# The first batch's x in whole-width loads, a quarter of the weights' conversion in the middle stage, and the last units' sums on VectorE

## The chip, the cores and the metric

The kernel runs on one core of a Trainium2 chip. The metric is the device time of one execution in microseconds (us); the median of several runs is given. The engines are called by the names that the profile uses: PE (the matrix multiplier), DVE (VectorE), ACT (ScalarE), POOL (GpSimd) and SP (the queue that issues most transfers). A line such as L545 is a line of the kernel's file.

## The reference

A global filter over the sequence, and then a two-layer network whose activation is h - tanh(h):

```python
# x (8, 3008, 256) f32; filt_r, filt_i (1505, 256) f32; w_in (256, 2048), w_out (2048, 256) f64
X = np.fft.rfft(x, axis=1)
y = np.fft.irfft(X * (filt_r + 1j * filt_i)[None], n=3008, axis=1).astype(np.float32)
x2 = y.reshape(8 * 3008, 256)
h = x2 @ w_in
g = h - np.tanh(h)
out = (g @ w_out).astype(np.float32)      # (24064, 256)
```

The weights come as 64-bit floats. The kernel reads them as pairs of 32-bit words and makes 32-bit floats of them by integer operations.

## The kernel before, in words

**The filter.** 3008 = 64 x 47, so a sequence position is 47 q + r with q of 64 and r of 47, and the two transforms become three stages of matmuls. The *first* stage is a 64-point transform over q, for each r (matmul `pf`, copied to `a`, written to a buffer `ct1` in device memory). The *middle* stage reads `ct1` back with r on the partitions (`a<-ct`), does the 47-point step (`pz`), multiplies by the filter (`uv`, `zs`, on DVE), goes back over r (`pe`, copied to `e1s`), and writes `ct2`. The *last* stage reads `ct2` (`e<-ct`) and does the 64-point step back (`pu`, copied to `ut`). The batches are handled in the units (0), (1,2), (3,4), (5,6), (7).

**The network.** Tokens are taken in 48 groups of up to 512, and each group in four units of hidden columns, 192 in all. Both matrix products are done with seven products of half-size blocks in place of eight (Strassen and Winograd), which needs sums of blocks on both sides. `combine` (L523 to L527) makes the four sums of a moving operand: for a group's `ut` it gives `tu`, for a unit's `h` it gives `t`. All its subtractions are on POOL, but for one of the last unit (L526), which is on DVE. `sums` (L257 to L263) makes the four sums of a quarter of a weight, on POOL. The hidden activation goes over ACT (L619 to L630) and DVE (L626, L633); `up`, `shrink` and `down` are the three steps of a unit, and PE's L545 and L680 are the products of the two layers. The main loop keeps PE full; the first and middle stages of the later batches are fitted into it by a list of due steps.

**The prologue.** Only batch 0's first and middle stage, the weights' conversion and the first group's last stage stand ahead of the main loop. The order of the work is that of the program, engine by engine (the scheduling is manual):

- On SP: the matrix `wf1`, the loads of x for r below 24 (`load_x0`, L873), matrices `fg`, then the raw weights. The loads of x for r from 24 on are issued by ACT. The one set of 64 rows lies on partitions 0 to 63, the other on 64 to 127, and a chunk holds eight r of each; the first chunk comes in two cuts.
- `first0` (L878 to L901) does the first stage for three chunks: a matmul over both halves with a block matrix of `wf1` (L891), a copy by ACT (L894), two writes to `ct1` by ACT (L898). In the last chunk the second half is one r shorter, so matmul and copy are split there, and the row that is missing is filled with zeros by POOL (`pad`, L945 to L947).
- `weights_alone` converts three quarters of a weight, two jobs each, all on DVE (L204 to L230), ahead of the middle stage in DVE's order. A job's load (`raw`, L197) is issued by SP; there are three buffers.
- The middle stage then goes through 16 steps of `j`. Each step also calls the generator `weights` once, which does six more jobs with two of the operations on ACT (L216, L217). At j = 13 two jobs of one more quarter are begun. What is left of the jobs is finished after the loop. The filter's rows come by POOL's loads (L910) and are doubled by ACT (L914, L915); `turned` (L923, L924) makes a second matrix on POOL.
- After the loop: `e2` is loaded, the remaining jobs are finished, `pu` and `ut` follow, then `tu`, and the first product L545.

**The end.** After the last unit's activation, `bounded` (L776 to L786) counts on DVE, from sums that the activation left, whether a bound held (`small`, L781; `least`, L783), and PE adds it up over the partitions (`pc`, L785). PE runs its queue in order, so what follows `pc` waits for `least`.

Of the kernel before, what the change touches and what calls it, by code (L numbers as in the profile page):

```python
# [9 lines left out]
F32 = mybir.dt.float32  # L10
# [12 lines left out]
NQ, NR = 64, 47  # L23
# [3 lines left out]
RP = 48  # L27
# [39 lines left out]
def _consts():  # L67
# [10 lines left out]

    wf1 = np.zeros((2, 128, 64, 2))
    for b in range(2):  # L80
        wf1[0, 64 * b:64 * b + 64, :, b] = f1
        wf1[1].reshape(128, 2, 64)[64 * b:64 * b + 64, b] = f1
# [47 lines left out]
    for b in range(2):  # L130
# [9 lines left out]
            for v in (wf1, fg.reshape(IM + RP, -1), s2, np.eye(128))]  # L140
# [3 lines left out]
def kernel(  # L144
# [11 lines left out]
    wf1_d, fg_d, s2_d, one_d = (  # L156
        nc.inline_tensor(v, name=n).ap() for v, n in zip(_consts(), ("wf1", "fg", "s2", "one")))
# [342 lines left out]
    def last(i, z):  # L500


        p, c = groups[i]
        ws_ = widths(p, c)
        n = sum(ws_)
        e2 = e2s.pop(i)
        ut = dn.tile([128, 2, CH * 128], F32, tag="ut", bufs=2, name="ut")
        for h in range(2):
            pu = z("pu", [128, CH * 128])
            for j, w in enumerate(ws_):  # L510
                nc.tensor.matmul(pu[:, j * 128:j * 128 + w], e2[0:w, j, h * 128:(h + 1) * 128],  # L511
                                 s2[0:w, 0:w], start=True, stop=True)
            ACT.copy(ut[:, h, 0:n], pu[:, 0:n])
            if h == 0:
                yield
        w = n // 2
        tu = dn.tile([128, 4, 256], F32, tag="tu", bufs=2, name="tu")
        b = [[ut[:, h, k * w:(k + 1) * w] for k in range(2)] for h in range(2)]
        combine(b, [tu[:, k, 0:w] for k in range(4)])
        uts[i] = (b, tu, w)  # L520
        yield

    def combine(b, t, shared=False):  # L523
        G.tensor_sub(t[0], b[0][1], b[0][0])  # L524
        G.tensor_sub(t[1], b[1][1], t[0])  # L525
        (V if shared else G).tensor_sub(t[2], b[1][1], b[0][1])  # L526
        G.tensor_sub(t[3], t[1], b[1][0])  # L527
# [79 lines left out]
    def shrink(U):  # L607
# [46 lines left out]
        combine(blocks, [t[:, k, :, 0:w] for k in range(4)], U + 1 == 4 * len(groups))  # L654
# [121 lines left out]
    def bounded(z):  # L776


        small = tr.tile([128, 2 * 4 * len(groups)], F32, tag="a2", bufs=2, name="small")
        least = cst.tile([128, 1], F32, name="least")  # L780
        V.tensor_single_scalar(out=small, in_=y_sums, scalar=float(np.arctan(S * NEAR) ** 2),  # L781
                               op=ALU.is_lt)
        V.tensor_reduce(out=least, in_=small, axis=mybir.AxisListType.X, op=ALU.min)  # L783
        pc = z("pc", [1, 1])
        nc.tensor.matmul(pc, least, ones, start=True, stop=True)  # L785
        V.tensor_copy(count, pc)  # L786

# [68 lines left out]
    with tc.tile_pool(name="tr", bufs=2) as tr, tc.manual_schedule():  # L856
        with tc.tile_pool(name="pro", bufs=1) as pro, \
# [11 lines left out]
            def load_x0(c, cuts=(0, 8)):  # L869
                t = big([128, 8, DM], F32, "x0")  # L870
                for lo, hi in zip(cuts, cuts[1:]):
                    for h, rows, r, n in halves(0, 8 * c + lo, hi - lo):
                        (nc.sync, ACT)[h].dma_start(  # L873
                            t[rows, lo:lo + n, :],
                            dram(x.tensor, r * DM, [[NR * DM, 64], [1, n * DM]]))
                return t

            def first0(xt, c):  # L878

                for i in range(2):  # L880
                    r = 8 * c + 4 * i
                    a1 = pro.tile([128, 4, DM], F32, tag="a1", bufs=4, name="a1")
                    parts = halves(0, r, 4)
                    m = parts[1][3]
                    for j in range(2):
                        pf = z0("pf", [128, 2, DM])
                        lo, mid, hi = 2 * j, max(2 * j, min(2 * j + 2, m)), 2 * j + 2
                        for rows, lo, hi in ((128, lo, mid), (64, mid, hi)):
                            if lo < hi:
                                to = pf[0:rows, lo - 2 * j:hi - 2 * j, :]  # L890
                                nc.tensor.matmul(to, wf1[0:rows, 1, 0:rows],  # L891
                                                 xt[0:rows, 4 * i + lo:4 * i + hi, :],
                                                 start=True, stop=True)
                                ACT.copy(a1[0:rows, lo:hi, :], to)  # L894
                        if j == 0:
                            yield
                    for _, rows, r_h, n_h in parts:
                        ACT.dma_start(  # L898
                            dram(ct1[0], r_h * 64 * DM, [[DM, 64], [64 * DM, n_h], [1, DM]]),
                            a1[rows, 0:n_h, :])  # L900
# [35 lines left out]
            nc.sync.dma_start(wf1, wf1_d)  # L936
# [28 lines left out]
            G.dma_start(s2, s2_d)  # L965
            turned(mats[0][1], gx[0])
# [7 lines left out]
            ws = weights(tiles0, range(3, 6), 2)  # L974
# [63 lines left out]
        with tc.tile_pool(name="dn", bufs=2) as dn, \  # L1038
# [42 lines left out]

            late, copies = weights_slow(tiles1, range(7, 8)), filters_d()
# [4 lines left out]
            for U in range(total + 2):  # L1087
# [120 lines left out]
```

## Time and profile before

| | us |
|---|---|
| median of 7 runs | 2805.2 (2804.85 to 2809.74) |
| the profiled execution | 2806.02 |
| its span | 2804.2 |
| PE busy in the span | 2719.7 (97%) |
| DVE busy | 1913.4 (68%) |
| ACT busy | 1885.6 (67%) |
| POOL busy | 1766.8 (63%) |

The span is what the profiler's records cover; the profiled execution is 1.8 us longer. The page gives the span in 40 slices of 70.1 us, in tenths of busy time. The mean granted clock of PE is 0.99 of full speed. The stretch ahead of PE's full load ends at about 126 us, and the span's last 10 us hold the last products, the transposes and the stores.

In the lines of a timeline the columns are start and duration in us, engine, line, operation, output and inputs, shapes and the number of merged instructions; what stands in brackets is how long the engine had been idle and what ended that. The chain of waits follows the work that ended last back to its start, here shown in the order of time.

### The profile page before, as it was taken

To read this page: it belongs to the slowest core of one execution; us is meant where nothing else is said; L and a number is where in the kernel's file an instruction comes from. 1 tells how busy PE (TensorE), PEld (TensorE's weight loads), DVE (VectorE), ACT (ScalarE), POOL (GpSimd) and SP (SyncE) were. 2 spreads that over 40 slices of the span, in tenths; PEclk is the share of its full clock that TensorE was granted. 3 is DMA by queue.
4 is the path that set the end of the run, shared out by engine and by line. 5 is a ranking of instruction groups with operands and counts; after the bars stand their busy time and mean duration, and the time that the engine had idled before them with its cause. 6 is when DMAs were issued, how large, how long until landed. Compare 5 with 4: busy or idle time off the path is not lost.

```text
span 2804.2 us, 36463 instructions
## 1 busy us (share of the span) xinstructions
PE 2719.7 (97%) x12438; PEld 2273.3 (81%) x12438; DVE 1913.4 (68%) x2175; ACT 1885.6 (67%) x2790; POOL 1766.8 (63%) x1407
## 2 busy tenths in 40 slices
PE   4899999999999999999999999999999999999998
PEld 2577778888888888888888888888888888898887
DVE  6755666656776777666677777766676676777776
ACT  2466777666767777666667777766666676666665
POOL 5546887544776777544586777654476666565655
PEclk7999999999999999999999999999999999999999
DMA  9854443332333322223333233112223222111010
GB/s 249 214 185 116 111 118 82 87 87 72 72 75 82 75 69 60 58 84 80 88 72 75 70 80 84 38 43 66 59 66 80 63 57 58 30 19 26 16 22 17
DMA packets 322592, 217.53 MB, mean 78 GB/s; under 512 B 224783, under 2 KB 274747, under 8 KB 322157
## 3 DMA queue, kind: packets, MB, share of 16 engines
q1 hardware_dynamic: 266826, 157.28, 24.1%
q10 hardware_dynamic: 52818, 51.53, 6.0%
q0 software_dynamic: 2752, 6.30, 0.8%
q8 instruction: 100, 1.64, 0.2%
q14 instruction: 96, 0.78, 0.1%
HBM read 138.87 MB, written 79.17 MB: 78 GB/s over the span
## 4 chain that ended last, share of the span: by engine, by line
PE 83%; DVE 6%; ACT 4%; issue 2%; DMA 2%; POOL 2%; ACTq 0%; DVEq 0%; SPq 0%; POOLq 0%
PE o L680 35%; PE x L545 21%; PE z L545 10%; PE y L545 5%; PE pe L411 3%; PE pz L430 3%; PE pu L511 3%; PE pf L351 2%; DVE h L626 2%; ACT y L622 1%; DMA raw<-in_moe_w_in_dram 1%; DVE h L596 1%; ACT y L619 1%; DMA a<-ct 1%; DVE h L633 0%
## 5 line engine op out<-in xcount | busy, mean ns | idle before, releaser
L626 DVE TENSOR_TENSOR h<-h,y 128x1024 f32<-128x1024 f32 (+2 forms) x384 | 578.1, 1505 | 311.4 <-ACT y L622 310.3
L680 PE MATMUL o<-t,wd 128*128 128x256 f32 (+2 forms) x3072 | 775.3, 375 | 1.8 <-POOL t L526 1.3
L680 PEld LDWEIGHTS o<-t,wd 128*128 128x128 f32 x3072 | 579.5, 190 | 93.8 <-issue 22.0
L633 DVE SCALAR_TENSOR_TENSOR h<-sq,h 128x1024 f32<-128x1024 f32 (+2 forms) x384 | 558.5, 1454 | 121.8 <-ACT sq L630 113.7
L524 POOL TENSOR_TENSOR t<-h 128x512 f32<-128x512 f32 (+2 forms) x192 | 240.2, 1251 | 553.3 <-DVE h L633 402.5
L680 PE MATMUL o<-h,wd 128*128 128x256 f32 (+2 forms) x2304 | 583.1, 376 | 4.0 <-DVE h L633 4.0
L545 PE MATMUL x<-tu,wu 128*128 128x256 f32 (+2 forms) x2304 | 582.0, 375 | 4.3 <-POOL tu L525 2.1
L545 PEld LDWEIGHTS x<-tu,wu 128*128 128x128 f32 x2304 | 430.4, 190 | 105.4 <-issue 42.9
L680 PEld LDWEIGHTS o<-h,wd 128*128 128x128 f32 x2304 | 430.7, 190 | 77.7 <-issue 15.8
L630 ACT ACTIVATE sq<-y,near_b 128x1024 f32<-128x1024 f32 (+2 forms) x384 | 435.0, 1133 | 6.4 <-DVE h L633 0.2
L619 ACT ACTIVATE y<-h 128x1024 f32<-128x1024 f32 (+2 forms) x384 | 397.4, 1035 | 14.4 <-ACT e L414 6.4
L622 ACT ACTIVATE y<-y 128x1024 f32<-128x1024 f32 (+2 forms) x384 | 399.9, 1041 | 6.6 <-ACT a L352 0.4
L551 ACT COPY s<-x 128x512 f32<-128x512 f32 (+2 forms) x192 | 110.8, 577 | 328.5 <-PE x L545 308.4
L527 POOL TENSOR_TENSOR t<-t,h 128x512 f32<-128x512 f32 (+2 forms) x192 | 319.0, 1662 | 0.1
L551 ACT COPY u<-x 128x512 f32<-128x512 f32 (+2 forms) x384 | 220.7, 575 | 138.2 <-PE x L545 119.8
L525 POOL TENSOR_TENSOR t<-h,t 128x512 f32<-128x512 f32 (+2 forms) x192 | 245.9, 1281 | 15.0
L526 POOL TENSOR_TENSOR t<-h 128x512 f32<-128x512 f32 (+2 forms) x191 | 245.7, 1286 | 0.0
L446 POOL TENSOR_TENSOR zs<-zs,ft 128x512 f32<-128x512 f32 x112 | 164.9, 1472 | 94.2 <-ACT zs L444 94.0
L447 POOL TENSOR_TENSOR uv<-uv,zs 128x512 f32<-128x512 f32 x112 | 206.7, 1845 | 9.1 <-DVE uv L445 0.5
L545 PE MATMUL x<-ut,wu 128*128 128x256 f32 (+2 forms) x768 | 198.5, 381 | 11.1 <-DVE h L596 8.3
L588 DVE TENSOR_TENSOR h<-z,u 128x512 f32<-128x512 f32 (+2 forms) x192 | 128.8, 671 | 112.6 <-ACT u L551 111.6
L545 PE MATMUL z<-tu,wu 128*128 128x256 f32 (+2 forms) x768 | 195.5, 377 | 0.0
(122 smaller groups left out, 3293.7 us busy)
## 6 DMA issues: line engine op xcount, KB each, us to landing
a<-ct SPq DMA_DIRECT2D x64, 384.0 KB, 4.0
ft<-filt SPq DMA_DIRECT2D x96, 256.0 KB, 4.7
out_dram<-ot SPq DMA_DIRECT2D x1392, 16.0 KB, 1.5
ct<-e ACTq DMA_DIRECT2D x112, 192.0 KB, 2.2
ct<-a ACTq DMA_DIRECT2D x80, 256.0 KB, 2.9
x_sb<-in_x_dram SPq DMA_DIRECT2D x69, 256.0 KB, 2.9
e<-ct SPq DMA_DIRECT2D x33, 512.0 KB, 4.2
fg<-fg SPq DMA_DIRECT2D x40, 392.0 KB, 4.9
```

The lines of the kernel that those rows point to most:

```text
L524: G.tensor_sub(t[0], b[0][1], b[0][0])
L525: G.tensor_sub(t[1], b[1][1], t[0])
L526: (V if shared else G).tensor_sub(t[2], b[1][1], b[0][1])
L527: G.tensor_sub(t[3], t[1], b[1][0])
L545: nc.tensor.matmul(bank[:, k], wu[:, q - 1, (2 * u + k) * 128:(2 * u + k + 1) * 128], rhs[q - 1], start=(first and k == 0), stop=True, ski ...
L551: ACT.copy(t, X)
L619: ACT.activation(y[k], ht[k], AF.Arctan, scale=S)
L622: ACT.activation(y[k], y[k], AF.Square, accum_out=y_sums[:, 2 * U + k // 2:2 * U + k // 2 + 1])
L626: V.tensor_mul(ht[k], ht[k], y[k])
L630: ACT.activation(sq[k], y[k], AF.Square, bias=near_b, scale=A)
L633: V.scalar_tensor_tensor(out=ht[k], in0=sq[k], scalar=K, in1=ht[k], op0=ALU.add, op1=ALU.mult)
L680: nc.tensor.matmul(product(q), wd[:, q - 1, (2 * u + k) * 128: (2 * u + k + 1) * 128], rhs[q - 1][:, k], start=(u == 0 and k == 0 and q == ...
```

## The change

Five edits:

1. Batch 0's x is loaded with 128 partitions in one transfer, all on SP: partition 2q + h holds eight r, from r = 8c for h = 0 and from 24 + 8c for h = 1. The last r of the second half (r = 47) is the first row of the next q. A new matrix `wf0` (64 KB, loaded in front) does the transform from that order; matmul and copy are not split any more, each `ct1` write has four r, and the zero padding with its transfer is left out (the rows are read by matmuls that leave that r out).
2. `wf1` is loaded by POOL's queue, behind `s2`.
3. `weights_alone` has two quarters (four jobs); the generator in the middle stage has four (eight jobs, 20 stops for the same 17 calls, and what is left follows after the loop).
4. `combine` takes its engine: DVE for the first group's `tu` and for the `t` of the last two units, POOL otherwise.
5. `bounded` is a generator: its DVE part is issued at the last unit's step k = 0, before `e()`, and the matmul with the count at k = 2.

```diff
+    wf0 = np.zeros((64, 2, 2, 64))
     for b in range(2):
+        wf0[:, b, b] = f1
...
-        combine(b, [tu[:, k, 0:w] for k in range(4)])
+        combine(b, [tu[:, k, 0:w] for k in range(4)], G if i else V)
...
-    def combine(b, t, shared=False):
-        G.tensor_sub(t[0], b[0][1], b[0][0])
-        G.tensor_sub(t[1], b[1][1], t[0])
-        (V if shared else G).tensor_sub(t[2], b[1][1], b[0][1])
-        G.tensor_sub(t[3], t[1], b[1][0])
+    def combine(b, t, by):
+        by.tensor_sub(t[0], b[0][1], b[0][0])
+        by.tensor_sub(t[1], b[1][1], t[0])
+        by.tensor_sub(t[2], b[1][1], b[0][1])
+        by.tensor_sub(t[3], t[1], b[1][0])
...
-        combine(blocks, [t[:, k, :, 0:w] for k in range(4)], U + 1 == 4 * len(groups))
+        combine(blocks, [t[:, k, :, 0:w] for k in range(4)],
+                G if U + 2 < 4 * len(groups) else V)
...
-    def bounded(z):
+    def bounded():
...
         V.tensor_reduce(out=least, in_=small, axis=mybir.AxisListType.X, op=ALU.min)
-        pc = z("pc", [1, 1])
+        yield
+        pc = z1("pc", [1, 1])
         nc.tensor.matmul(pc, least, ones, start=True, stop=True)
         V.tensor_copy(count, pc)
+        yield
...
                 for lo, hi in zip(cuts, cuts[1:]):
-                    for h, rows, r, n in halves(0, 8 * c + lo, hi - lo):
-                        (nc.sync, ACT)[h].dma_start(
-                            t[rows, lo:lo + n, :],
-                            dram(x.tensor, r * DM, [[NR * DM, 64], [1, n * DM]]))
+                    nc.sync.dma_start(
+                        t[:, lo:hi, :],
+                        dram(x.tensor, (8 * c + lo) * DM,
+                             [[NR * DM, 64], [HALF * DM, 2], [1, (hi - lo) * DM]]))
...
                     for j in range(2):
                         pf = z0("pf", [128, 2, DM])
-                        lo, mid, hi = 2 * j, max(2 * j, min(2 * j + 2, m)), 2 * j + 2
-                        for rows, lo, hi in ((128, lo, mid), (64, mid, hi)):
-                            if lo < hi:
-                                to = pf[0:rows, lo - 2 * j:hi - 2 * j, :]
-                                nc.tensor.matmul(to, wf1[0:rows, 1, 0:rows],
-                                                 xt[0:rows, 4 * i + lo:4 * i + hi, :],
-                                                 start=True, stop=True)
-                                ACT.copy(a1[0:rows, lo:hi, :], to)
+                        nc.tensor.matmul(pf, wf0, xt[:, 4 * i + 2 * j:4 * i + 2 * j + 2, :],
+                                         start=True, stop=True)
+                        ACT.copy(a1[:, 2 * j:2 * j + 2, :], pf)
...
-                    for _, rows, r_h, n_h in parts:
+                    for h in range(2):
                         ACT.dma_start(
-                            dram(ct1[0], r_h * 64 * DM, [[DM, 64], [64 * DM, n_h], [1, DM]]),
-                            a1[rows, 0:n_h, :])
+                            dram(ct1[0], (r + HALF * h) * 64 * DM,
+                                 [[DM, 64], [64 * DM, 4], [1, DM]]),
+                            a1[64 * h:64 * h + 64])
...
-            nc.sync.dma_start(wf1, wf1_d)
+            wf0 = pro.tile([128, 128], F32, name="wf0_sb")
+            nc.sync.dma_start(wf0, wf0_d)
...
-            ws = weights_alone(tiles0, range(3))
-
-            pad = pro.tile([64, DM], F32, name="pad")
-            G.memset(pad, 0.0)
-            G.dma_start(dram(ct1[0], NR * 64 * DM, [[DM, 64], [1, DM]]), pad)
+            ws = weights_alone(tiles0, range(2))
...
             G.dma_start(s2, s2_d)
+            G.dma_start(wf1, wf1_d)
...
-            ws = weights(tiles0, range(3, 6), 2)
+            ws = weights(tiles0, range(2, 6), 2)
...
+            bound = bounded()
...
+                        if U == total + 1 and k in (0, 2):
+                            next(bound)
                         e()
                         t(k)
-                        if U == total + 1 and k == 0:
-                            bounded(z1)
```

More of the change, by code (lines that the diff above doesn't have):

```diff
@@ L139, in _consts @@
     return [np.ascontiguousarray(v, dtype=np.float32)
-            for v in (wf1, fg.reshape(IM + RP, -1), s2, np.eye(128))]
+            for v in (wf0.reshape(128, 128), wf1, fg.reshape(IM + RP, -1), s2, np.eye(128))]
 @with_exitstack
@@ L155 @@
     V, G, ACT = nc.vector, nc.gpsimd, nc.scalar
-    wf1_d, fg_d, s2_d, one_d = (
-        nc.inline_tensor(v, name=n).ap() for v, n in zip(_consts(), ("wf1", "fg", "s2", "one")))
+    wf0_d, wf1_d, fg_d, s2_d, one_d = (
+        nc.inline_tensor(v, name=n).ap()
+        for v, n in zip(_consts(), ("wf0", "wf1", "fg", "s2", "one")))
     ct1 = [nc.dram_tensor(f"ct1_{p}", (RP, 64 * len(bs), DM), F32, kind="Internal")
@@ L882, in first0 @@
                     a1 = pro.tile([128, 4, DM], F32, tag="a1", bufs=4, name="a1")
-                    parts = halves(0, r, 4)
-                    m = parts[1][3]
                     for j in range(2):
                         pf = z0("pf", [128, 2, DM])
-                        lo, mid, hi = 2 * j, max(2 * j, min(2 * j + 2, m)), 2 * j + 2
-                        for rows, lo, hi in ((128, lo, mid), (64, mid, hi)):
-                            if lo < hi:
-                                to = pf[0:rows, lo - 2 * j:hi - 2 * j, :]
-                                nc.tensor.matmul(to, wf1[0:rows, 1, 0:rows],
-                                                 xt[0:rows, 4 * i + lo:4 * i + hi, :],
-                                                 start=True, stop=True)
-                                ACT.copy(a1[0:rows, lo:hi, :], to)
+                        nc.tensor.matmul(pf, wf0, xt[:, 4 * i + 2 * j:4 * i + 2 * j + 2, :],
+                                         start=True, stop=True)
+                        ACT.copy(a1[:, 2 * j:2 * j + 2, :], pf)
                         if j == 0:
                             yield
-                    for _, rows, r_h, n_h in parts:
+                    for h in range(2):
                         ACT.dma_start(
-                            dram(ct1[0], r_h * 64 * DM, [[DM, 64], [64 * DM, n_h], [1, DM]]),
-                            a1[rows, 0:n_h, :])
+                            dram(ct1[0], (r + HALF * h) * 64 * DM,
+                                 [[DM, 64], [64 * DM, 4], [1, DM]]),
+                            a1[64 * h:64 * h + 64])
                     yield
```

## The prediction

> **What bounds the kernel now.** I read the page's busy shares and its chain first, then the chain of waits over the first 150 us, the timelines of the engines there, the table by stretches of the same time, and last the timeline of the end.
>
> The page (busy us; the chain's shares by engine):
>
> ```profile
> PE 2719.7 (97%) x12438; PEld 2273.3 (81%) x12438; DVE 1913.4 (68%) x2175; ACT 1885.6 (67%) x2790; POOL 1766.8 (63%) x1407
> PE   4899999999999999999999999999999999999998
> PE 83%; DVE 6%; ACT 4%; issue 2%; DMA 2%; POOL 2%; ACTq 0%; DVEq 0%; SPq 0%; POOLq 0%
> ```
>
> PE is full but for the first slices (70 us each: 4 tenths, 8 tenths) and the last. What the change does in between shifts nothing; a microsecond is won or lost only before PE's full stretch begins (about 126 us) or after 2778 us. Both ends are what the diff edits. The chain of waits of the first stretch (start, us, what):
>
> ```profile
> 1.18 5.74 DMA x<-in_x_dram
> 6.94 15.14 DMA raw<-in_moe_w_in_dram
> ...
> 39.35 9.25 DMA raw<-in_moe_w_in_dram
> 51.48 6.25 DMA a<-ct
> ...
> 79.75 9.47 DMA a<-ct
> ...
> 120.26 0.84 DVE wd L230 x3
> ...
> 125.25 0.79 POOL tu L525
> 126.09 1.13 PE x L545 x4
> ```
>
> The chain goes through the conversions on DVE, then the middle stage's loads, then conversions, then the sums of `tu` on POOL; only there does PE get its first product. DVE's timeline (start, us, line) shows what holds the first filter multiply L1011:
>
> ```profile
> 41.43 0.42 DVE L204 TENSOR_SCALAR conv<-raw 128x512 int32<-128x512 int32 x1
> 41.77 0.95 DVE L205 TENSOR_SCALAR conv<-raw 128x512 int32<-128x512 int32 x1
> 48.63 0.43 DVE L204 TENSOR_SCALAR conv<-raw 128x512 int32<-128x512 int32 x1 [0.86 <-DMA raw<-in_moe_w_in_dram]
> 52.77 0.68 DVE L1011 TENSOR_TENSOR uv<-pz,filt 128x512 f32<-128x512 f32 x1
> ```
>
> The six jobs of `weights_alone` start at 22.26, 26.41, 30.54, 37.28, 41.43 and 48.63, and the first `uv` is queued behind the sixth, though its first load of `a` has landed by 43.2 us. A job takes 4.15 us, but 6.3 to 6.7 where POOL's sums run beside it: the 0.42 us op takes 0.95. Stretches (us; last two columns the share of the DMA engines and GB/s):
>
> ```profile
> 7.00:15.00 8.00, 5.96 (x8) 2.06 (x8) 0.00 (x0) 2.25 (x4) 4.88 (x7) 1.00 1.02 252
> 60.00:70.00 10.00, 8.43 (x37) 5.91 (x36) 8.60 (x17) 6.54 (x9) 9.83 (x15) 1.00 0.72 198
> 70.00:80.00 10.00, 8.86 (x40) 6.51 (x39) 9.32 (x17) 6.31 (x10) 8.28 (x13) 1.00 1.06 257
> ```
>
> The DMA engines are full in most of this part, so DVE's early freedom can be taken back by transfers. PE's timeline at the end:
>
> ```profile
> 2783.95 1.40 PE L680 MATMUL o<-t,wd 128*128 128x224 f32 x6 [1.30 <-POOL t L526]
> 2785.88 1.02 PE L680 MATMUL o<-t,wd 128*128 128x224 f32 x4 [0.53 <-POOL t L527]
> 2790.56 0.19 PE L785 MATMUL pc<-ones,least 128*1 128x1 f32 x2 [1.95 <-DVE least L783]
> ```
>
> PE waits there for POOL's sums of the last but one unit and for the bound's count: 3.78 us in three waits.
>
> **The change part by part.** Sums are against the profiled execution, 2806.02 us (span 2804.2), 0.8 us above the median of 2805.2.
>
> 1. x over 128 partitions, all on SP. The same bytes (3.1 MB; 64 KB of matrix in place of 128 KB ahead of them, the 128 KB now on POOL's queue later). Two SP issues and four ACT issues become four SP issues of about 0.95 us (3.82 us for four), so SP reaches the raw loads at the same 6.9 us, and ACT is free 2.6 us earlier, when it had 4.2 us of idle time. I keep the rate of 252 GB/s. Then only bytes help: 64 KB of matrix and 64 KB of pad less, 64 KB more of x (row 47 of the second half): raw0, and the first job with it, 0.3 us earlier. Bounds: 3.2 us earlier, were x moved at the 339 GB/s of the 22 to 30 us stretch (12.3 us for 3.1 MB becomes 9.1); 12 us later, were one queue given half of 252. I take the value nearest to the row of x itself.
>  [...]
> 2. Unsplit matmuls and copies in the first stage, two whole ct writes, no pad memset or pad DMA. L894's pieces of 0.36 us and one pair of short matmuls go, off the chain. What ACT waits for there, 2.73 and 2.90 us "<-DMA raw", comes from issue waits of its ct writes on earlier transfers and depends on which loads precede. With x on SP the last ct write goes out about 5 us earlier than 33.65, at 28 to 29, if they follow raw; the first `a` load then lands at about 38 (43.2 before), an estimate with the same 9.6 us from write to landing. Nothing gained by itself: it is next in line after DVE.
> 3. Four jobs instead of six ahead of the middle. The fifth and sixth, 41.43 to 52.77, go: 11.3 us. First `uv` at 52.77 - 11.3 - 0.3 = 41.2. If `a` is not earlier, it is 43.5 and the gain 9.3; the conversion's POOL sums (3.3 us a group) are also one group fewer there.
> 4. Eight jobs instead of six inside the middle. The generator has 20 stops for 17 calls, so per step the same work is done, and the rhythm of two steps (pairs at 60.66, 67.52, 74.20: 6.8 us, POOL 9.83 of 10 busy) stands. But raw loads and filters that moved before 52.77 must now move after 41.2: 1.1 MB more backlog, 4.3 us at 257 GB/s, against 2.8 us of idle DMA at 60 to 70 and 5.7 at 100 to 113. I take 2.5 us lost; bounds 0 (the idle time swallows it) and 8 (below, rival B).
> 5. After the last `zs` (110.04) DVE had 2.0 us of first ops, waited 3.88 for ACT's L216 and finished two jobs in 2.6 us each, at 121.09. Now it has the last two jobs' finishes too (2 x 2.6), the wait shrinks under them: 12.9 us for 11.05 to 11.3, 1.6 lost. Bounds: 0, and 5.2 if the wait stays.
> 6. `tu` on DVE. POOL did it behind its sums of wd (121.17 to 124.49), at 124.49 and 125.25, PE at 126.09, 4.8 us after `ut`. On DVE, four ops of 0.42 to 0.69 follow `ut` directly: first product at ut + 2.7, 2.1 us won; bounds 0 (if DVE's next conversion's 0.95 us ops stand first) and 3.
> 7. wf1 from POOL behind s2: one issue of 0.6 us on POOL's queue at about 34, where `turned` and the filter loads stand behind it; POOL then idles 1.36 and 7.91 us, which hides it. The matrix is used from 126 us on. Cost nothing; without that cover, 0.6.
> 8. The end. The last but one unit's sums start when DVE is through with L604 (2779.2) and take 4 x 0.62, ready at 2781.7 for 2785.8: both PE waits, 1.83 us, go. DVE's next L626 moves from 2779.80 to 2781.7, but the 1.85 to 2.02 us that L633 and L626 took beside POOL return to 1.09; the last h is ready at about 2786.1 (2786.77), and the last sums, 4 x 0.62, at 2788.6 (2790.9). The count's wait of 1.95 goes, as the matmul is asked two steps later. With the last 11 matmul groups of 4.05 us behind 2788, PE ends at about 2792.0 for 2794.73: 2.7 won. Bounds 1 (DVE's 2.5 us push the last h back) and 4.
>
> Sum: -0.3 - 11.3 + 2.5 + 1.6 - 2.1 = -9.6 at the start, -2.7 at the end: -12.3, so 2793.7 against the profiled run and 2792.9 against the median. I forecast 2793.
>
> **Rivals.** B: transfers take most of it back. Up to the pu at 118.6 us, 28.7 MB pass, 242 GB/s on the mean; the full stretches run at 252 to 339, those of 70 to 100 us at 263. To save 10 us the mean must be 264. At 250 the start gains 118.6 - 116 = 2.6 us; with the end, 5.5: about 2799.5. For it: three of the chain's pieces are loads. Against it: 2.8 and 5.7 us of idle engines named above.
> C, slower: ACT's ct writes and SP's loads wait on each other's completions. Before, one pair does this (ACT's write at 89.29 late, then a pair of 9.5 us from 82.51 to 92.00 instead of 6.8): 2.7 us each. With another order of loads other pairs can fall so. To end 0.2% slower, 17.9 us must be lost, that is seven of eight pairs; from five on, the kernel is about unchanged. For it: ACT's L216 shows 2.28 "<-DMA a<-ct". Against: it happened once in eight. Time at seven pairs: 2793 + 18.9 = 2812.
> D, the merge does harm: one queue for x at half the rate, first job 12 us later, the gain of step 3 gone: about 2805. Against it: the page's SP queue alone moved 59.5% of all DMA time to 60 us.
>
> **How the numbers follow.** Changes under 0.2% (5.6 us) can hardly be told from none. Forecast 62%; B 22%, of which 6 end within 0.2%; C 9%, of which 2 do; D 7%, of which a half true leaves 3 faster, 2 the same and 2 slower. Faster: 62 + 16 + 3 = 81%. Same: 6 + 2 + 2 = 10%. Slower: 7 + 2 = 9%. The forecast's own bounds, adding the likelier ones of steps 1, 4, 6 and 8, give 2786 to 2799; B reaches to 2803. Range 2785 to 2803.
>
> **What would show it.** First `uv` (L1011) at 41 us and `a` landed by 39; four jobs ahead of it. Last `zs` at 100 to 101; pairs of 7 us. First product L545 behind `tu` at 115 to 117, released by DVE and no longer by POOL. At the end no PE wait for POOL's sums, none for `least`, the last L680 some 3 us earlier against the start of the last unit. Wrong if raw0 lands after 24 us, if pairs take 8 us or more, if SP's loads stand behind a raw load that waits for a late L223, or if L626 of the last unit becomes the end's wait.

## The result, and the profile after

The changed kernel takes 2799.33 us (median of 14 runs, 2797.57 to 2801.73) against 2805.74 for the kernel before beside it: a ratio of 0.9976, 95% interval 0.9970 to 0.9983. It is 6.4 us faster. The forecast was 12.3 us, so about half of it did not come. The profiled execution took 2799.61 us, with a span of 2797.8 for 2804.2.

The page of the kernel after; the same three lines as of before:

```profile
PE 2721.0 (97%) x12436; PEld 2273.6 (81%) x12436; DVE 1905.5 (68%) x2182; ACT 1889.3 (68%) x2793; POOL 1756.7 (63%) x1395
PE   5899999999999999999999999999999999999998
PE 82%; DVE 7%; ACT 4%; issue 2%; POOL 2%; DMA 2%; ACTq 0%; SPq 0%; DVEq 0%; POOLq 0%
```

Only the first slice has one more tenth of PE. The chain of waits of the first stretch (start, us, what):

```profile
1.18 4.18 DMA x<-in_x_dram
5.38 15.84 DMA raw<-in_moe_w_in_dram
...
45.94 9.16 DMA filt<-in_filt_r_dram
...
60.91 14.12 DMA raw<-in_moe_w_out_dram
...
81.13 7.58 DMA filt<-in_filt_r_dram
...
95.54 1.17 PE pe L989 x2
...
116.64 0.83 DVE wd L234 x3
120.87 2.08 PE x L549 x4
```

The conversions on DVE now end at 40 us and not at 52. In their place stand loads that were issued inside the middle stage and took 7.6 to 14.1 us, two of them POOL's small filter loads. The stretches from 7 us on (last three columns: PE's granted clock, the share of the DMA engines, GB/s):

```profile
7.00:15.00 8.00, 5.67 (x11) 2.26 (x10) 0.00 (x0) 2.25 (x4) 3.67 (x6) 1.00 1.02 275
60.00:70.00 10.00, 6.74 (x27) 4.16 (x25) 8.35 (x17) 4.97 (x7) 6.28 (x10) 0.97 1.07 250
70.00:80.00 10.00, 8.98 (x33) 6.59 (x34) 6.93 (x14) 4.49 (x6) 9.51 (x15) 0.83 1.08 255
```

The slack of 0.72 that the kernel before had between 60 and 70 us is gone: the DMA engines are full from 38 to 90 us, at shares of 1.01 to 1.08. DVE's timeline, the first `uv`, the start of the last pair of steps, and the last `zs`:

```profile
40.37 0.68 DVE L1013 TENSOR_TENSOR uv<-pz,filt 128x512 f32<-128x512 f32 x1
101.78 0.69 DVE L1013 TENSOR_TENSOR uv<-pz,filt 128x512 f32<-128x512 f32 x1 [2.62 <-ACT filt L918]
105.06 0.68 DVE L1014 TENSOR_TENSOR zs<-pz,filt 128x512 f32<-128x512 f32 x1
```

The kernel before ends its middle stage, begun at 52.77, with

```profile
109.36 0.68 DVE L1012 TENSOR_TENSOR zs<-pz,filt 128x512 f32<-128x512 f32 x1
```

The last pair starts 10.2 us after the one before it (91.57). In one table, from the timelines of the two profiled executions:

| us | before | after | difference | forecast |
|---|---|---|---|---|
| first `uv` starts | 52.77 | 40.37 | -12.4 | -11.6 |
| first `uv` to last `zs` | 56.6 | 64.7 | +8.1 | +2.5 |
| last `zs` to `ut` | 12.0 | 15.2 | +3.2 | +1.6 |
| `ut` to the first product of the second layer | 30.0 | 28.2 | -1.8 | -2.1 (as `tu`) |
| from there to the last unit but one's second-layer products | 2627.5 | 2626.4 | -1.1 | 0 |
| from those to the end of the span | 25.4 | 23.0 | -2.5 | -2.7 |
| sum | | | -6.5 | -12.3 |

Of the 12.4 us won ahead of the middle stage, 11.3 are lost again before `ut`. The start and the end came as forecast; the 1.1 us of the main loop were not forecast, and nothing here explains them. The question is what took the 8.1 and the 3.2.

The tables by stretches from the first `uv` to the end of the last `zs` say that it is not more work: DVE was busy for 45.9 us before and 45.8 after, ACT for 29.5 and 31.4, POOL for 49.0 and 47.4, and PE, with 47.5 and 51.8, was full in neither. The bytes are more: 13.4 MB before and 15.3 after, at 234 and 235 GB/s.

### The profile page after: what moved, and what is told of

It reads as the page before. It is cut to its first block, busy times and chain, and to the rows that moved or that the text cites. A ratio compares the mean times of both kernels' runs of the same rounds, so it can differ in the third digit from the quotient of the medians.

```text
span 2797.8 us, 36449 instructions
## 1 busy us (share of the span) xinstructions
PE 2721.0 (97%) x12436; PEld 2273.6 (81%) x12436; DVE 1905.5 (68%) x2182; ACT 1889.3 (68%) x2793; POOL 1756.7 (63%) x1395
## 3 DMA queue, kind: packets, MB, share of 16 engines
q8 instruction: 100, 1.64, 0.3%
## 4 chain that ended last, share of the span: by engine, by line
PE 82%; DVE 7%; ACT 4%; issue 2%; POOL 2%; DMA 2%; ACTq 0%; SPq 0%; DVEq 0%; POOLq 0%
PE o L686 35%; PE x L549 21%; PE z L549 10%; PE y L549 5%; PE pe L415 3%; PE pz L434 3%; PE pu L515 3%; PE pf L355 2%; DVE h L630 2%; ACT y L626 1%; DVE h L600 1%; DMA filt<-in_filt_r_dram 1%; DVE h L637 1%; ACT y L623 1%; DMA raw<-in_moe_w_in_dram 1%
## 5 line engine op out<-in xcount | busy, mean ns | idle before, releaser
L630 DVE TENSOR_TENSOR h<-h,y 128x1024 f32<-128x1024 f32 (+2 forms) x384 | 571.5, 1488 | 311.8 <-ACT y L626 310.4
L637 DVE SCALAR_TENSOR_TENSOR h<-sq,h 128x1024 f32<-128x1024 f32 (+2 forms) x384 | 557.6, 1452 | 124.6 <-ACT sq L634 117.0
L623 ACT ACTIVATE y<-h 128x1024 f32<-128x1024 f32 (+2 forms) x384 | 397.4, 1035 | 15.2 <-ACT e L418 6.4
L626 ACT ACTIVATE y<-y 128x1024 f32<-128x1024 f32 (+2 forms) x384 | 399.9, 1041 | 6.6 <-ACT a L356 0.4
L549 PE MATMUL x<-ut,wu 128*128 128x256 f32 (+2 forms) x768 | 199.5, 382 | 10.8 <-DVE h L600 8.3
L549 PE MATMUL y<-ut,wu 128*128 128x256 f32 (+2 forms) x768 | 194.6, 376 | 0.0
```

What stands on the lines that cost most here:

```text
L549: nc.tensor.matmul(bank[:, k], wu[:, q - 1, (2 * u + k) * 128:(2 * u + k + 1) * 128], rhs[q - 1], start=(first and k == 0), stop=True, ski ...
L623: ACT.activation(y[k], ht[k], AF.Arctan, scale=S)
L626: ACT.activation(y[k], y[k], AF.Square, accum_out=y_sums[:, 2 * U + k // 2:2 * U + k // 2 + 1])
L630: V.tensor_mul(ht[k], ht[k], y[k])
L637: V.scalar_tensor_tensor(out=ht[k], in0=sq[k], scalar=K, in1=ht[k], op0=ALU.add, op1=ALU.mult)
```

## The experiments

The first theory: transfers bound the middle stage, so that what is saved ahead of it is spent in it, and each other part is worth what its stretch shows. The rival: what one queue issues waits by chance for another queue's loads, and the order of the loads decides. The trace of the kernel before has such waits: two of ACT's copies in the first stage came 2.73 and 2.90 us late, behind issues of ACT that raw loads of SP released. That completions are shared is the author's reading of them and not shown.

### One part undone at a time

Three quarters ahead again:

```diff
-            ws = weights_alone(tiles0, range(2))
+            ws = weights_alone(tiles0, range(3))
...
-            ws = weights(tiles0, range(2, 6), 2)
+            ws = weights(tiles0, range(3, 6), 2)
```

> The kernel after, with six conversion jobs ahead of the middle stage again (three quarters, as before); all other edits stay. Theory (transfers bound the middle stage, so what is saved ahead of it is spent inside it): the first uv goes from 40.4 to about 51.5 us, the middle gets 7 to 8 us shorter (from 64.7 us between first uv and last zs to about 57), the tail about 2 us; total within 2 us of the kernel after, 2799 to 2801. Reckoning of the prediction: the part is worth 11.3 - 2.5 - 1.6 = 7.2 us, so 2806.5. Rival (completions that happen to be shared): another order gives another set of stalls, the total may go either way by 5 us, with the middle's pairs irregular.

Measured: 2800.02 us (before beside it 2805.2; ratio 0.9983, 0.9974 to 0.9992), 0.7 slower than the kernel after, less than the two intervals can part. DVE's timeline of this run:

```profile
50.53 0.68 DVE L1013 TENSOR_TENSOR uv<-pz,filt 128x512 f32<-128x512 f32 x1
107.85 0.68 DVE L1014 TENSOR_TENSOR zs<-pz,filt 128x512 f32<-128x512 f32 x1
```

The middle takes 57.3 us again, and `ut` comes 11.7 us after the last `zs`. The quarter moved into the middle stage wins 10.2 us at the first `uv`, costs 7.4 in the middle and 3.5 behind it, and is worth nothing that can be measured. The theory's outcome stands, and the prediction's step 4 falls; what in the middle takes the time this run does not tell.

The end undone:

```diff
-                G if U + 2 < 4 * len(groups) else V)
+                None if U + 1 == 4 * len(groups) else G)
...
+        by, by2 = by or G, by or V
...
-        by.tensor_sub(t[2], b[1][1], b[0][1])
+        by2.tensor_sub(t[2], b[1][1], b[0][1])
...
-                        if U == total + 1 and k in (0, 2):
-                            next(bound)
                         e()
                         t(k)
+                        if U == total + 1 and k == 0:
+                            for _ in bound:
+                                pass
```

> The kernel after, with the end as before: the last but one unit's sums on POOL, three of the last unit's four sums on POOL, and the count's matmul at once behind the DVE part. Theory (the end is worth 2.5 us, the difference between the shift of the end of the span, 6.4, and the shift of the loop ahead of it, 3.9): 2801.8, with PE waits for POOL's sums back near 1.3 and 0.5 us. Rival (PE has slack there, and the end's gain belongs to the clock or to the store): 2799.3, no change.

Measured: 2803.74 us (0.9993, 0.9984 to 1.0002), 4.4 slower than the kernel after. PE's timeline has the three waits of before to the hundredth:

```profile
2778.10 1.40 PE L687 MATMUL o<-t,wd 128*128 128x224 f32 x6 [1.30 <-POOL t L531]
2780.03 1.02 PE L687 MATMUL o<-t,wd 128*128 128x224 f32 x4 [0.53 <-POOL t L532]
2784.72 0.19 PE L793 MATMUL pc<-ones,least 128*1 128x1 f32 x2 [1.95 <-DVE least L790]
2786.14 4.43 PE L687 MATMUL o<-t,wd 128*128 128x224 f32 x14
```

In the kernel after there is one wait instead, of 1.82 us for the last unit's h, and none for the count. In the profile of before the product on `h` behind the count's matmul starts at 2790.68 us, though `h` was ready at 2786.77; in the kernel after the count is asked later and nothing stands behind a wait for it:

```profile
2782.22 2.16 PE L686 MATMUL o<-h,wd 128*128 128x224 f32 x10 [1.82 <-DVE h L637]
2786.96 0.19 PE L792 MATMUL pc<-ones,least 128*1 128x1 f32 x2
```

The last 14 matmuls took 4.43 us here and 2.81 in the profile of before, which has the same waits. The table by stretches of this run shows why: the granted clock was 0.66 from 2786 to 2791 us, where the kernel before has 1.00 over the same matmuls (2791.8 to 2796.9). From the second layer's products of the last unit but one to the end of the last product it is 13.3 us in the kernel after, 16.0 before and 17.6 here. So in the profiles the end is worth 2.7 us, and 4.4 in the execution in which PE's clock fell. That the median's 4.4 comes from such falls is not shown: the profiled execution, which has one, took 2801.94 us, less than the median. The theory's 2.5 had the waits and the direction right.

`tu` on POOL:

```diff
-        combine(b, [tu[:, k, 0:w] for k in range(4)], G if i else V)
+        combine(b, [tu[:, k, 0:w] for k in range(4)], G)
```

> The kernel after, with the first group's tu on POOL again. Theory of the prediction: 2.1 us slower, 2801.4. Rival (PE takes its products on ut first, and what follows waits for the activation, not for tu): within 0.7 us of the kernel after, 2799 to 2800.

Measured: 2798.66 us (0.9977, 0.9968 to 0.9986), 0.7 faster than the kernel after: the outcome of the rival, no effect. PE's timeline of the kernel after:

```profile
117.23 2.53 PE L515 MATMUL pu<-s_sb,e 128*128 128x128 f32 x16 [3.87 <-DMA e<-ct]
120.87 2.08 PE L549 MATMUL x<-ut,wu 128*128 128x256 f32 x4 [1.10 <-ACT ut L517]
122.74 1.91 PE L549 MATMUL y<-ut,wu 128*128 128x256 f32 x4
124.44 1.51 PE L549 MATMUL x<-tu,wu 128*128 128x256 f32 x4
```

The two products on `ut` that PE takes first cost 2.08 and 1.91 us, against 1.13 and 1.03 in the kernel before, so `tu` is ready before PE is. But half clock is not the reason that the move wins nothing. The run with the old end also has `tu` on DVE, PE was at full clock there (1.13 and 1.03 us for the same two products), and its timelines of PE and DVE have:

```profile
122.68 1.11 PE L550 MATMUL x<-tu,wu 128*128 128x256 f32 x4
125.52 1.12 PE L355 MATMUL pf<-x_sb,wf_sb 128*128 128x512 f32 x2 [1.73 <-DVE h L576]
```

```profile
124.78 0.68 DVE L576 TENSOR_TENSOR h<-y,s 128x512 f32<-128x512 f32 x1
```

PE takes its product on `tu` at once and then waits 1.73 us for `h`, which stands on DVE behind the four sums of `tu` and three operations of a conversion. Six profiles with `tu` on DVE have this wait, of 1.64 to 1.74 us. Counted from the start of `ut`, `h` starts after 4.6 us with `tu` on DVE and after 3.7 with it on POOL, where in turn the product on `tu` starts only after 4.6. The `pf` behind both starts after 5.3 us in the run with the old end, 5.6 in the kernel after and 5.6 with `tu` on POOL. What the move takes from one wait it adds to another.

The same stretch of the kernel after by the table:

```profile
120.00:124.00 4.00, 3.13 (x7) 2.52 (x8) 3.05 (x5) 1.66 (x3) 3.35 (x4) 0.50 0.86 198
```

The clock was 0.50 there. PE had waited 3.87 us for `e` before 117.23, and the table gives 1.00 from 113 to 118 us, 0.65 from 118 to 120, then 0.50, and 1.00 again from 126. The kernel before has the same dip, at 0.50 from 128 to 130 us, behind waits of 1.34 us for `ut` and 2.14 for `tu`; and in the run with `gx` on ACT (below) a wait of 3.81 us for `e` brought none: the 16 products of `pu` behind it took 2.02 us, as in the kernel before at a clock of 1.00, against 2.53 in the kernel after. What sets the clock is not shown here.

The dips also show where the stretch behind `ut` won its 1.8 us. The same product, in the kernel before and in the kernel after:

```profile
128.42 1.91 PE L545 MATMUL z<-tu,wu 128*128 128x256 f32 x4
126.65 1.03 PE L549 MATMUL z<-tu,wu 128*128 128x256 f32 x4
```

With the `pf` on each side of it, that is 1.57, 1.91 and 1.36 us before and 1.02, 1.03 and 1.02 after, 1.8 us in all. In the run with `tu` on POOL these three are short too, so it is not that move that shifted the dip.

x loaded as before, with all other parts kept (the diff against the kernel after is the load, `first0`, the pad and `wf1` of the change, undone):

> The kernel after, with x loaded as before in halves by SP and ACT, the split first stage and the pad; wf1 again first on SP. Theory (bytes and their order are nearly the same): the first job starts at about 22.3 instead of 21.2, the first uv at 41.5; the 1.1 us goes through or is swallowed by the middle: 2799.3 to 2800.5. Rival (shared completions): the order of the loads differs by the ACT loads of x and the pad, so the stalls in the middle fall elsewhere and the total moves by 3 us or more in either direction.

Measured: 2801.57 us (0.9984, 0.9975 to 0.9993), 2.2 slower than the kernel after: more than the theory's range and less than the rival's 3, with first job at 21.96, first `uv` at 41.54 and a middle of 65.3. The table of this run, to set beside the row of 275 above:

```profile
7.00:15.00 8.00, 7.55 (x11) 3.03 (x12) 0.00 (x0) 2.34 (x4) 4.88 (x7) 1.00 1.06 267
```

The four profiles with x in halves have 251 to 267 GB/s from 7 to 15 us, when x and the first raw loads move, and the first job at 21.96 to 22.26; the ten with whole loads have 273 to 295, and the first job at 20.05 to 21.20. Earlier, from 5 to 7 us, the difference is larger: 270 GB/s in the kernel before, 352 in the kernel after. The four issues of x on SP took 2.7 us in the kernel after in place of 3.8, and SP began to issue the raw loads at 4.6 us in place of 6.9. No run parts the higher rate from the earlier issue. The merge is worth 0.8 to 2.2 us at the first job, and 1.2 at the first `uv` of this run; that this passes through to the end fits the 2.2, which is within its uncertainty.

### What fills the middle stage

Half of the bytes in the conversions' loads: 64 partitions instead of 128 for the ten jobs inside and behind the middle stage, in the kernel after and in the kernel before. The other half of these weights is left out of the result.

```diff
+        m = 64 if half and not alone else 128
+        src = bass.AP(tensor=src.tensor, offset=src.offset,
+                      ap=[[src.ap[0][0], m]] + [list(v) for v in src.ap[1:]])
+        t = t[0:m]
...
-        it, pt, st = (tiles(k, I32, n) for k in ("it", "pt", "st"))
-        ft = tiles("ft", F32, n)
+        it, pt, st = (tiles(k, I32, n)[0:m] for k in ("it", "pt", "st"))
+        ft = tiles("ft", F32, n)[0:m]
...
+            V.memset(wu[64:128], 0.0)
+            V.memset(wd[64:128], 0.0)
```

> The kernel after, with the ten conversion jobs inside and behind the middle stage on 64 partitions only: each raw load has 256 KB in place of 512 KB, with the same number and order of transfers and of engine operations (their time goes by the free size). The other half of these weights is set to zero once at the start, on DVE while it idles; so this part of the weights is left out of the result. Theory (bytes bound the middle): 2.0 MB fewer in the middle stage, 8 us at 250 GB/s; first uv unchanged at 40.4, middle from 64.7 to about 57 us, total 2791 to 2793. Rival (shared completions and POOL's queue, not bytes): pairs stay at 8 to 10 us, total 2797 to 2800.

> The same halving in the kernel before: eight jobs inside and behind the middle stage. Theory (bytes): the middle before had slack in the transfers (shares 0.72 and 0.56 in two stretches) and loses less: 57.3 us to about 54, total 2801 to 2803. Rival: no change, 2804 to 2806.

Measured: after 2798.55 us (0.9975, 0.9966 to 0.9985), middle 64.5 us; before 2807.29 (1.0005, 0.9996 to 1.0014), middle 57.6, with its first `uv` at 55.2, behind a load that came 3.53 us late. Neither got faster by what can be measured. DVE's operations on 64 partitions took as long as on 128 (0.41 us and 0.68, against 0.42 and 0.68). The bytes of these loads alone do not bound the middle. PE's timeline of the halved kernel shows where it stands instead:

```profile
94.47 1.17 PE L998 MATMUL pe<-zs,gx 112*96 112x256 f32 x2 [5.28 <-POOL gx L935]
```

Another order of the loads: one of 256 bytes more.

```diff
+            shift = pro.tile([1, 64], F32, name="shift")
+            nc.sync.dma_start(shift, wf0_d[0:1, 0:64])
```

> The kernel after with one more load of 256 bytes on SP ahead of the middle stage. [...] Theory (bytes): within 1 us, 2798.5 to 2800.5, the two waits of 2.26 and 3.38 us of ACT gone or elsewhere but the middle as long, as the transfers stay full. Rival (shared completions): these two waits go or others come, and the total moves by 3 us or more.

Measured: 2798.58 us (0.9977, 0.9968 to 0.9986), within a microsecond. ACT's waits of 2.26 and 3.38 us, which the kernel after has for `fg` and a raw load, are gone from its timeline, and the middle is no shorter (66.5 us, in the slowest execution of this run, 2802.80). The rival of chance falls: these waits were there and cost nothing that shows. The long last pair is still there (14.7 us), and PE waits 7.00 us in it for POOL's `gx`. POOL's timeline of the kernel after, in the same place:

```profile
89.92 0.51 POOL L914 DMA_DIRECT2D filt<-in_filt_i_dram  x1 [0.43 <-DMA filt<-in_filt_i_dram]
90.50 0.73 POOL L264 TENSOR_TENSOR wu<-wu 128x256 f32<-128x256 f32 x1
94.25 1.24 POOL L928 TENSOR_SCALAR gx<-fg 48x384 f32<-48x384 f32 x1
96.11 1.17 POOL L928 TENSOR_SCALAR gx<-fg 48x384 f32<-48x384 f32 x1
```

`gx` stands in POOL's queue behind the issues of filter loads, which wait for earlier filter loads (10.5 us in 12 waits from 38 to 105 us), and behind a quarter's sums. That made a new theory: POOL's queue in order sets the middle. The test takes `gx` off POOL, in both kernels:

```diff
-                G.tensor_copy(t[0:RP], g3[IM:IM + RP])
-                G.tensor_scalar_mul(t[IM:IM + RP], g3[0:RP], -1.0)
+                ACT.copy(t[0:RP], g3[IM:IM + RP])
+                ACT.mul(t[IM:IM + RP], g3[0:RP], -1.0)
```

> The kernel after, with the two operations of turned (gx, L927 and L928) on ACT in place of POOL; nothing else. POOL then has 13 us less work between the first uv and the last zs, and PE's pe no longer stands behind POOL's issues of filter loads, which wait for earlier loads on that queue. Theory (POOL's queue in order sets the middle: 48 us of work and 10.5 us of waits for filter loads without another gap): the long last pairs, 10 to 15 us in all kernels with four jobs ahead, go back to 7 to 8, no PE wait for gx; middle from 64.7 to 57 to 60 us, total 2793 to 2796. Rival (bytes, or ACT becomes the bound with 8 us more): middle 63 us or longer, total 2798 to 2801.

> The kernel before with the same edit. There POOL idled 7.9 us ahead of the first uv, and its filter loads were ahead of their use; theory: little to win, middle 56.6 to 54 to 56, total 2803 to 2805. Rival (the edit helps of itself, whatever stands ahead of the middle): as much as in the kernel after, 4 us or more, 2801 or less.

Measured: after 2796.16 us (0.9964, 0.9952 to 0.9977), middle 61.8; before 2801.83 (0.9987, 0.9978 to 0.9996), middle 52.3. The two middle stages with `gx` on ACT, first `uv` and last `zs` of the kernel after and of the kernel before:

```profile
39.35 0.68 DVE L1013 TENSOR_TENSOR uv<-pz,filt 128x512 f32<-128x512 f32 x1
101.15 0.68 DVE L1014 TENSOR_TENSOR zs<-pz,filt 128x512 f32<-128x512 f32 x1
53.04 0.68 DVE L1011 TENSOR_TENSOR uv<-pz,filt 128x512 f32<-128x512 f32 x1
105.34 0.68 DVE L1012 TENSOR_TENSOR zs<-pz,filt 128x512 f32<-128x512 f32 x1
```

The edit is worth 3.2 us in the kernel after and 4.4 in the kernel before: the rival of the second run. So POOL's queue costs time in both, and is not what the change lost: with `gx` on ACT in both, the middle with four jobs ahead is 9.5 us longer than with six. My theory of POOL falls as the cause. The long last pairs are gone (6.5 us), and PE's timeline of the kernel after with this edit has another wait:

```profile
71.67 2.05 PE L1006 MATMUL pz<-a,fg 94*128 94x256 f32 x4 [4.99 <-DMA fg<-fg]
```

Both together, halved loads and `gx` on ACT:

> The kernel after with both edits: the raw loads inside and behind the middle stage halved (half of these weights is left out of the result, set to zero) and turned on ACT. Theory (two bounds lie side by side in the middle, the transfers and POOL's queue, and each hides what is taken from the other alone): halving alone gave 64.7 to 64.5, turned alone 64.7 to 61.8; both together give more than the sum, middle 54 to 57 us, no PE wait for fg of more than 2 us in all, total 2788 to 2791. Rival (the bytes never mattered, and what is left after POOL is the latency of the loads' chain): middle 60.5 to 62 us, total 2794 to 2797.

Measured: 2792.87 us (0.9944, 0.9931 to 0.9958), middle 59.5. That lies between the two brackets. The two edits alone took 0.2 and 2.9 us from the middle, together 5.2. That each hides a part of the other would fit, but is not shown: profiles of kernels with the same code in the middle have 63.3 (`tu` on POOL) to 66.5 us (the extra load). And 7.2 us more than the 52.3 of the kernel before with `gx` on ACT are left; the kernel before with both edits was not run. Its table, and POOL's first wait in the middle:

```profile
70.00:80.00 10.00, 8.41 (x31) 5.91 (x30) 8.54 (x16) 6.84 (x11) 6.99 (x12) 0.83 0.99 217
80.00:90.00 10.00, 7.77 (x33) 5.12 (x32) 8.32 (x17) 8.34 (x13) 6.64 (x12) 1.00 1.02 220
```

```profile
52.45 0.54 POOL L921 DMA_DIRECT2D filt<-in_filt_r_dram  x1 [4.01 <-DMA filt<-in_filt_r_dram]
```

The DMA engines are as full as with whole loads (0.99 and 1.02) but move 217 and 220 GB/s where the same stretches of the run with `gx` on ACT alone moved 247 and 256, at shares of 1.05 and 1.01. A share of 1 did not mean that bytes were the limit: half a load took less than half out of the engines' time. Filter loads took 8.4 us from issue to landing (median; 6.5 in the kernel before), and POOL waited 15.7 us in all for them.

Set beside the kernel before, this run has much the same traffic in its middle: 13.6 MB from 38 to 100 us, added up from the table by stretches, at a share of 0.98, against 13.4 MB in the 57.3 us from the first `uv` to the end of the last `zs` in the kernel before, at 0.92. `gx` on ACT changes no load, so about 13.4 MB are also what the kernel before moved with it, in 53.0 us (an estimate from the bytes of the kernel before). So the bytes do not make the remaining 7 us. **What stays open**: why the same traffic takes longer, and whether the latency of the chains of small loads is what PE and DVE then wait for. No run here changed the filter loads alone.

### The tail, and the two together

The seventh quarter's conversion goes out of the tail into the main loop's slow generator; then the same with `gx` on ACT:

```diff
-                    ws_gap = weights(tiles0, range(6, 7), 2)
-                    next(ws_gap)
...
-            for w in (ws, ws_gap):
-                for _ in w:
-                    pass
+            for _ in ws:
+                pass
...
-            late, copies = weights_slow(tiles1, range(7, 8)), filters_d()
+            late, copies = weights_slow(tiles1, range(6, 8)), filters_d()
```

> The kernel after with the two jobs of the seventh quarter (first begun at step 13 and finished behind the middle stage) moved into the slow generator of the main loop, which so far has the eighth quarter. Theory (the tail behind the last zs is a chain of conversions on DVE): the tail loses two starts of 1.3 to 2.5 us and two finishes of 2.6 us: last conversion from 119.9 to about 111, then the e loads (landed by 117.2) and pu bound; 4 to 6 us faster than the kernel after, 2793 to 2795. Rival (the loads of e and of raw bound the tail): the first product moves by 2 us or less, 2797 to 2799; or the sums of the last quarters come late in the main loop and cost PE waits there.

> The kernel after with turned on ACT and the seventh quarter's conversion in the main loop's slow generator. Theory: both shares add, as one acts in the middle and the other in the tail behind it: middle 57 to 60 us, tail 11 to 12 us in place of 15 from last zs to ut; 2788 to 2792. Rival (e's load bounds the tail, 10.4 us from last zs to ut as in the run without the edit on ACT, so only the middle's share counts): 2792 to 2795.

Measured: 2795.87 us (0.9966, 0.9952 to 0.9980) and 2790.94 us (0.9947, 0.9934 to 0.9961). The tail from last `zs` to `ut` is 10.4 and 10.3 us in place of 15.2. In the first run, whose profiled execution was its slowest (2800.81, with a middle of 67.7 us), the last conversion ends at 113.17 and `ut` starts at 117.86: `e`'s load is next in line, as the rival had it, so the gain is 3.5 us and not 4 to 6. In the second the middle is 61.7 us, not the 57 to 60 of the expectation, and the total came into its range by the tail. It is the fastest kernel of the study, 0.53% under the kernel before.

## Why the prediction was half right

- **Step 1**, x in whole loads: forecast 0.3 us, measured 1.1 in the profile and 0.8 to 2.2 over the runs. Keeping the rate of the row was wrong: from 5 to 7 us 352 GB/s moved, as in the bound of 3.2, where the kernel before has 270; but from 9 to 13 us it was 244 to 260 again, and most of the bound did not come. The trace of the kernel before has four issues of x on SP, not two; with whole loads four take 2.7 us and not 3.8, so SP reached the raw loads at 4.6 us and not at the same 6.9.
- **Steps 2 and 3**, the first `uv`: forecast 41.2, measured 40.37. The balance of DVE with the loads of `a` was right: PE's `pz` was released by `a` at 37.36.
- **Step 4** failed. It took 2.5 us for the backlog, with bounds of 0 and 8; the middle lost 8.1. The step reckoned bytes over a rate and then filled the DMA engines' idle time with them, and it let the pairs stand at 6.8 us. But that rhythm was read from three pairs: the seven spacings of the kernel before are 6.7 to 9.5 us, 7.7 on the mean. In the kernel after they are 7.4 to 10.8, 8.8 on the mean; pairs of 8 us or more, which the prediction named as a sign of being wrong, did come. The loads' latency grew with them (filter loads 6.5 to 7.9 us, `a` 10.2 to 14.8, as medians), and small loads sit in chains (filter loads of 9.16 and 7.58 us in the chain above). That the moved quarter brings the loss is shown by the run with three quarters ahead; by which wait it does so stays open.
- **Rival B** had the right total, 2799.5 for 2799.33, and the right place, in part by luck. Its mean rate of 250 GB/s is in the rows (238 to 258 from 38 to 90 us), but the runs with halved loads show that bytes alone are not what counts. Its gain at the start has a slip: 28.7 MB at 250 GB/s are 114.8 us and not 116, so 3.8 us won and not 2.6; `pu` came 1.4 us earlier, and 2.9 came from the two later stretches that it did not name.
- **Step 5** was half of what came: 1.6 against 3.2 us. The starts of the last two jobs (L208 to L211, 4.2 us beside POOL's sums) followed the finishes and were not hidden. The bound was 5.2.
- **Step 6** fell: `tu` on DVE is worth nothing. The step ended at the product on `tu` and left out PE's next wait, for `h`, which on DVE stands behind the sums of `tu`. The 1.8 us that the stretch behind `ut` gained stays in each run that undid a single part, so no part is shown to be its cause; its place is in the timelines: three matmul groups of 1.57, 1.91 and 1.36 us in the kernel before, at clocks of 0.85, 0.50 and 0.80 from 126 to 132 us, that take 1.02 to 1.03 in the kernel after, where the clock was 1.00 from 126 us on.
- **Step 7**, `wf1` on POOL's queue: the issue took 0.58 us at 33.61, behind which nothing waited that shows. As forecast.
- **Step 8** was right: 2.7 us from the products of the last unit but one to the end of the last product (15.96 to 13.26), forecast 2.7. L626 and L633 of the last unit, L630 and L637 now, returned to 1.08 to 1.09 us from the 1.83 to 2.02 that they took beside POOL's sums; POOL was idle there. One sign of being wrong came with it: PE waits 1.82 us for the last unit's h.
- **Rivals C and D**: C's waits appeared (2.26 and 3.38 us on ACT) and vanished with another order without a change of time. D did not happen: with x on the single queue 275 GB/s moved from 7 to 15 us, for 252 before.

By the medians against the kernel after, undoing parts costs 0.7 (the quarter), 4.4 (the end), -0.7 (`tu`) and 2.2 us (x), each with some 2.5 us of uncertainty. That the sum, 6.6, is so near to the 6.4 that the change won is in part luck: by the ratios to the kernel before beside each, the parts are 2.0, 4.8, 0.3 and 2.2, with a sum of 9.3. The largest edit is worth nothing that can be measured, the end carries most of the gain, and the share of x is within its uncertainty.

## What to carry to other kernels

When work is moved out from ahead of a stage, ask what loads were landing under it: the wait on an engine was also the time in which the next stage's loads came in. Bytes over the mean rate did not give the loss here, so look at the moved stage's loads chain by chain too, with the latency that they have in a full stretch; and do not credit idle slices of the DMA engines to loads that are issued late. When an operation moves to an engine with less to do, ask what stands behind it there: `tu` left one wait and made another. Undoing one edit at a time is cheap, and here it showed that the largest edit had won nothing that can be measured.

## What the runs showed of the hardware

- With x in 128-partition loads on one queue the DMA engines moved 352 GB/s from 5 to 7 us (the kernel after), and 273 to 295 from 7 to 15 (ten profiles); with pairs of 64-partition loads on two queues 270 (the kernel before) and 251 to 267 (four profiles). Width and number of queues changed together.
- Loads on 64 partitions in place of 128 left the DMA engines as busy (shares of 0.99 to 1.05, for 1.01 to 1.07), at 217 to 244 GB/s for 247 to 256 between 50 and 90 us (`gx` on ACT in both).
- PE's clock did not fall at a fixed time after a wait. Behind four waits of 3.3 to 4.0 us for `e`, the 16 products of `pu` took 3.76 us (`tu` on POOL, the clock at 0.97 from 110 to 114 us and 0.50 from 114 to 120, the wait's end at 114.6), 3.59 (old x), 2.53 (the kernel after, where the clock was 1.00 from 113 to 118 us and 0.65 from 118 to 120, the wait's end at 117.2) and 2.02 (`gx` on ACT). At a clock of 1.00, in the kernel before, they took 2.02.
- After waits of 1.3, 0.5 and 1.95 us at the end the clock fell to 0.66 in one profile (14 matmuls in 4.43 us, the run with the old end) and stayed at 1.00 in another (2.81, the kernel before).
